# Sliding-window attention and Fourier mixing: the last chunk of the query-key projection at another rate, split straight from PSUM, and the first output-projection sets staged differently

## The chip, the cores and the metric

The kernel runs on one core of a Trainium2 chip. The metric is the device time of one execution in microseconds. PE is TensorE (matmuls; PEld its weight loads), ACT is ScalarE, DVE is VectorE, POOL is GpSimd, SP is SyncE, on whose queue all the DMAs named below are issued, in program order.

## The reference, cut to what matters

Four layers in turn on x (2048 x 640): attention, Fourier mixing, attention, Fourier mixing, each on a layer-normalized x and added to it.

```python
qkv = (x @ wqkv).reshape(B, S, 3, H, Dh)          # H = 32 heads, Dh = 20
scores = einsum("bhqd,bhkd->bhqk", q, k) * (Dh ** -0.5)
mask = (i - j >= 0) & (i - j < 256)
p = softmax(where(mask, scores, -1e9)); o = einsum("bhqk,bhkd->bhqd", p, v)
x = x + o.reshape(B, S, D) @ wo
...
y = dft_seq_re @ (x @ dft_hid_re.T) - dft_seq_im @ (x @ dft_hid_im.T); x = x + y
```

The change touches the attention layers alone, both of them alike.

## The kernel before, in words

Most large products are made with split operands: a float32 number becomes hi (rounded to the matmul type) plus lo (the rest), and three matmuls hi x hi, hi x lo, lo x hi make one product. `split` (L158) writes hi by ScalarE (L160) and lo by VectorE or GpSimd (L166).

**Head loop.** `heads` (L522) runs steps -10 to 128. Eight "quads" of four heads have 16 steps each, one for each block of 128 rows. A step makes four score products for the row maxima (`s_head`, L553, ten steps ahead: s = step + 10), whose masked maximum VectorE takes in place in PSUM (L558, three banks in turn), and four transposed score products (`t_head`, L578), which ScalarE turns into exponentials (L587) and GpSimd masks (L593, L597). `pv` (L608) multiplies the previous step's exponentials by the values. Every fourth step (94, 98, 102 and so on) `m_rows` transposes the maxima of four blocks, ScalarE copies them to `mt` (L567), and two small DMAs put them as row 61 into `qp` (L569), one tick later. The t_heads of the step four later are the first to need them. A step has two halves (z = 0, 1), and `tick` closes each: what was put off with `post(n, ...)` is issued n ticks later, what was put off with `defer(n, ...)` n steps later. Ticks set the order of the program only; the engines then run as their semaphores allow.

**Filler.** In the first half of a step `fill` (L671) puts in matmul pairs of other work, in this order:

- `project` (L490): the query and key projection, ten chunks of 128 columns. From step 0 on a chunk is made in two sets of two 512-column pieces, each set 30 pairs of matmuls with 64 rows (`lockstep`, L191). A chunk has 4 x 15 = 60 pairs, all ten 600. `fill` takes nf pairs a step, rounded so that a group of 15 comes out even; nf is RATE = 3.5, or more where a due time asks for it. `due` (L643) lists for each quad the pairs that must be done by a value of s; for the last quad 570 by s = 104 and 600 by s = 112. Quads are then loaded from DRAM by `pack` (L504), three DMAs a step.
- A finished piece is copied by ScalarE from PSUM (L477), cast and subtracted by GpSimd (L478, L479), and stored to DRAM (L456, 512 KB) six ticks after the copy.
- When the projection is at its end, `partials` (L852): the output projection for the first three of five chunks of the attention output (EARLY = 3; chunks 0 and 1 are heads 0 to 15, chunk 2 heads 16 to 23), 16 row blocks of 18 pairs (L191 again, 320 columns), nf = LATE = 9, so one block in two steps. It starts only when `early_o[0]["left"]` is 0. In the last steps and behind the loop the same work is made with full matmuls (`in_turn`, L173).

**Staging of the output projection.** `prepare(0)` runs ahead of the last chunk's first set: it loads the three weights. `prepare(2)` runs ahead of its second set: it splits them (hi on ScalarE, lo on GpSimd, 640 columns wide) and starts `load_o` (L743) for the first block of 512 rows. `load_o` loads a chunk of the attention output (L756, 256 KB) and, for a new range of heads, the reciprocal sums (L762, `rr`), posts GpSimd's scaling (L779) seven ticks later and the cut into hi and lo (L773) four ticks after that. `others` (L830) looks each step whether quad 5 has been stored and then loads chunks 1 and 2. `prepare(4)`, at the end of the projection, starts loading `y` (x in blocks of 128 x 640, L850), one a step for four steps. `stored` is set for a quad 14 ticks after its last pv.

**Behind the loop** the remaining partial products, then the last two chunks (`late`, L922), whose sums VectorE adds (L967), follow.

Of the kernel before, what the change touches and what calls it, by code (L numbers as in the profile page):

```python
# [7 lines left out]
F32 = mybir.dt.float32  # L8
# [9 lines left out]
P = 128  # L18
S = 2048
D = 640  # L20
# [6 lines left out]
NCH = 2 * D // P  # L27
# [6 lines left out]
EARLY = 3  # L34
AHEAD_X = 4
AFTER = 4
RATE = 3.5
FIRST = 7
LATE = 9
PACE = 0.65  # L40
SOON = 3
# [13 lines left out]
def cuts(ap, n):  # L55

    return [ap[:, i:i + n] for i in range(0, ap.shape[1] - n + 1, n)]
# [6 lines left out]
class Net:  # L64
# [66 lines left out]
    def next(self, name):  # L131
        i = self.turn.get(name, 0)
        self.turn[name] = i + 1
        tiles = getattr(self, name)[:3]
        return tiles[i % len(tiles)]
# [323 lines left out]
    def pieces(self, c, sbs, role):  # L459

        w = self.turn["w", c]
        sets, of = [], {}
        for sb in sbs:
            xt = self.xnt(sb)
            if sb % 2 == 0:
                sets.append(([], []))
            p = self.bank(role)
            of[id(p)] = p, sb, self.last_bank
            sets[-1][0].append(p)
            sets[-1][1].append([((w[:, 0, k, :], w[:, 1, k, :]), (xt[:, 0, k, :], xt[:, 1, k, :])) for k in range(KC)])  # L470

        lead = self.lead

        def copied(p, sb):
            st = self.work.tile([P, 2, 512], F32R, name="c", tag="c", bufs=3)
            r = self.raw()[:, :512]
            self.nc.scalar.activation(r, p, AF.Copy)  # L477
            self.post(1, lambda: self.nc.gpsimd.tensor_copy(st[:, 0, :], r))  # L478
            self.post(2, lambda: self.nc.gpsimd.tensor_tensor(  # L479
                out=st[:, 1, :], in0=r, in1=st[:, 0, :].bitcast(F32), op=OP.subtract))  # L480
            self.post(3 if lead else 6, lambda: self.store_qk(c, sb, st))
        for r in self.lockstep(sets):
            if isinstance(r, tuple):
                for p in r[1]:
                    p, sb, k = of[id(p)]
                    self.heavy.append((k, lambda p=p, sb=sb: copied(p, sb)))
                r = 0
            yield r
# [33 lines left out]
    def heads(self, xsrc, xdst, hook):  # L522
# [169 lines left out]
        for step in range(-LEAD, steps + 1):  # L692
            now[0] = step
            self.wide, self.lead, self.tiled = step + LEAD > steps, step < -2, step < steps - 1
            for f in later.pop(step, []):
                f()
            s, t, v = step + LEAD, step, step - 1
            if due and s >= due[0][0]:
                while done[0] < due[0][1]:
                    fill(15)  # L700
                due.pop(0)
                q, j = (s + AHEAD) // 16, (s + AHEAD) % 16 // 4
                for i, f in enumerate(self.pack(q, j)):
                    defer(i // 3, f)
                for f in later.pop(step, []):
                    f()
            if v >= 0 and v % 4 == 3:
                load_v(v // 4 + 2)
            if done[0] < total:
                nf = max([FIRST if t < 0 else RATE]  # L710
                         + [(d - done[0]) / max(1, at - s) for at, d in due])
            elif made[0] < early:
                nf = LATE
            else:
                nf = LATE
            rows = ((s - 1) // 16, ((s - 1) % 16) // 4) if 4 <= s < steps + 4 and s % 4 == 0 else None
            for z in range(2):
                for e in range(2):
                    heads = [(t_head, t, e), (s_head, s, 1 - e)]
                    for head, n, i in heads[::-1] if e else heads:  # L720
                        if 0 <= n < steps:
                            head(n // 16, n % 16, z, i)
                if 0 <= t < steps:
                    for e in range(2):
                        t_exp(t // 16, t % 16, z, e, e + 1)
                    t_mask(t // 16, t % 16, z)
                if z:
                    relieve()
                    if 0 <= v < steps:
                        pv(v // 16, v % 16)  # L730
                    if rows:
                        m_rows(*rows)
                if z == 0 and t >= 0 or t < -1 or t >= steps:
                    fill(nf)
                self.tick()
            if step > 16 * (NQ - 1):
                self.poll_late(step - 16 * (NQ - 1))
# [5 lines left out]
    def load_o(self, o, sb, k, raw=None, rr=None):  # L743
# [41 lines left out]
        if after:  # L785
            self.post(6, lambda: self.held.append(scale))
        else:
            self.post(7 if k < EARLY else 4 if sb == 2 else 6, scale)

    def let_go(self):  # L790
        held, self.held = self.held, []
# [16 lines left out]
    def prepare(self, n):  # L808

        nc, a = self.nc, self.a  # L810
        ks = range(EARLY)
        if n == 0:
            self.early_w = []
            raws = cuts(self.work.tile([P, 2 * D], F32, name="we", tag="wc"), D) + [None]
            self.early_l = [self.load_w(self.early_w, a["wo"], [k], at=k, eng=nc.gpsimd, into=raws[k]) for k in ks]
            for f in self.early_l:
                next(f)
        elif n == 2:
            self.take_big(0)
            self.early_w += pairs(cuts(self.big[0], D))[:EARLY]  # L820
            next(self.early_l[2])
            for i in range(2):
                self.defer(2 + 2 * i, lambda i=i: next(self.early_l[i]))
            self.take_big(1)
            oc = cuts(self.big[1], 512) + cuts(self.big[0][:, 6 * D:], 512)
            self.early_o = [dict(zip(ks, pairs(oc[:6]))), dict(zip(ks, pairs(oc[6:])))]
            self.early_o[0]["left"] = EARLY - 1
            self.load_o(self.early_o[0], 0, 0)

            def others():  # L830

                if (CHUNKS[EARLY - 1][1] // 4 - 1, 0) not in self.stored:
                    self.defer(1, others)
                    return
                for k in range(1, EARLY):
                    self.early_o[0]["left"] -= 1
                    self.load_o(self.early_o[0], 0, k)
            self.defer(1, others)
        elif n == 4:
            self.take_big(2, F32)  # L840
            for i in range(AHEAD_X):
                if i == 0:
                    self.load_y([i])
                else:
                    self.defer(i, lambda i=i: self.load_y([i]))
# [6 lines left out]
    def partials(self, xsrc):  # L852
# [4 lines left out]
        for t in range(NB):  # L857
# [3 lines left out]
            if i == 0:  # L861
                self.complete(sets[sb % 2])
            if sb + 1 < NSB and i == 0:
                for k in range(2):
                    self.load_o(sets[(sb + 1) % 2], sb + 1, k)
            ps = [self.bank("w" if self.wide else "m", 320) for _ in range(2)]
            terms = [self.out_terms(sets[sb % 2], w, ks, i, hf) for hf in range(2)]
            if self.tiled:
# [858 lines left out]
```

## Time and profile before

| | us |
|---|---|
| median of 3 runs (2180.86 to 2181.6) | 2180.93 |
| the profiled execution | 2180.11 |
| its span, first to last instruction | 2178.4 |

Mean granted TensorE clock of the profiled execution: 0.997. A row of the busy time by stretch reads: the stretch from the span's start and its length, then for PE, PEld, DVE, ACT and POOL the busy us with the number of instructions in brackets, then the granted clock, the mean busy share of the 16 DMA engines and their GB/s. Where it is asked for one line of code alone, only the engines that run that line have a column. A row in order of time reads: start, duration, engine, line, operation, output <- input, number merged, and in square brackets the idle time of the engine ahead of it with what ended it. A row of a group reads: line, engine, operation, output <- input, shapes, count | busy us, mean ns of one | idle us ahead of them, and what ended it.

### The profile page before, as it was taken

The numbers are of one execution on the slowest core, as the hardware profiler recorded it, in microseconds if no ns is written. First come the engines' busy times: TensorE is split into PE (matmuls) and PEld (weight loads), VectorE is DVE, ScalarE is ACT, GpSimd is POOL, SyncE is SP. The second block draws the span as 40 slices with busy tenths as digits, with TensorE's granted clock in tenths as the row PEclk, the third lists the DMA queues.
The fourth block names the chain that finished last, engine by engine and source line by source line (L and its number), as shares of the span: only waits on it lengthen the run. The fifth ranks groups of instructions, "written<-read, shape, count | busy, mean of one in ns | idle before, by whom it ended". The sixth has DMA issues, their size and how long they took to land.

```text
span 2178.4 us, 49193 instructions
## 1 busy us (share of the span) xinstructions
PE 2123.0 (97%) x17893; PEld 1777.4 (82%) x17893; DVE 1615.0 (74%) x3933; ACT 1150.3 (53%) x2483; POOL 930.8 (43%) x1458
## 2 busy tenths in 40 slices
PE   7999999899999999999999999998999999999999
PEld 7987777687878888889999877776877788888899
DVE  6348788786897868777751578886868878687777
ACT  3117777766554545543431277776665545455522
POOL 3037777875514223230130477777754333331300
PEclk9999999999999999999999999999999999999999
DMA  5546666786435454657646466667753454546653
GB/s 184 176 154 189 202 183 213 219 221 212 134 119 175 138 185 129 216 192 264 218 135 190 152 200 185 201 203 219 226 188 134 131 187 137 164 148 217 219 175 126
DMA packets 221618, 395.40 MB, mean 182 GB/s; under 512 B 39360, under 2 KB 85952, under 8 KB 221376
## 3 DMA queue, kind: packets, MB, share of 16 engines
q1 hardware_dynamic: 221376, 392.26, 57.0%
q8 instruction: 141, 2.31, 0.5%
q14 instruction: 101, 0.83, 0.1%
HBM read 273.94 MB, written 117.05 MB: 179 GB/s over the span
## 4 chain that ended last, share of the span: by engine, by line
PE 81%; DVE 6%; POOL 5%; ACT 4%; issue 2%; DMA 2%; SPq 0%; ACTq 0%; DVEq 0%; POOLq 0%
PE banks L1266 27%; PE banks L173 14%; PE banks L191 13%; PE banks L608 8%; PE banks L578 6%; PE banks L1521 6%; PE banks L553 4%; POOL big L166 1%; POOL ou L1196 1%; DVE qp L166 1%; ACT big L928 1%; PE banks L273 1%; DVE pt L1197 1%; POOL rs L978 1%; PE banks L565 1%
## 5 line engine op out<-in xcount | busy, mean ns | idle before, releaser
L558 DVE CUSTOM_DVE_ANT_0 banks<-banks,mask 128x384 f32<-128x384 f32 (+2 forms) x1024 | 526.8, 558 | 157.9 <-PE banks L553 119.3
L587 ACT ACTIVATE pt<-banks 128x384 f32<-128x384 f32 (+2 forms) x1024 | 430.5, 470 | 179.3 <-PE banks L553 95.4
L578 PE MATMUL banks<-qp,kp 61*128 61x384 f32 (+2 forms) x1024 | 310.6, 370 | 14.5 <-DMA qp<-mt 7.8
L593 POOL TENSOR_SCALAR_AFFINE_SELECT pt<-pt 128x256 f32<-128x256 f32 x512 | 212.8, 416 | 183.5 <-ACT pt L587 133.2
L553 PE MATMUL banks<-kp,qp 60*128 60x384 f32 (+2 forms) x1024 | 280.2, 360 | 1.4 <-DVE mc L558 1.1
L191 PE MATMUL banks<-big,wc 64*128 64x512 f32 x1920 | 269.6, 394 | 0.4 <-DVE pt L374 0.4
L578 PEld LDWEIGHTS banks<-qp,kp 61*128 61x128 f32 x1024 | 175.2, 185 | 79.9 <-ACT pt L587 35.3
L608 PE MATMUL banks<-pt,vq 128*32 128x128 f32 x5760 | 214.9, 278 | 2.9 <-POOL pt L593 2.9
L191 PEld LDWEIGHTS banks<-big,wc 64*128 64x128 f32 x1920 | 183.0, 185 | 28.0 <-ACT x L477 5.2
L608 PEld LDWEIGHTS banks<-pt,vq 128*32 128x32 f32 x5760 | 144.0, 109 | 57.5 <-issue 51.5
L597 POOL TENSOR_SCALAR_AFFINE_SELECT pt<-pt 128x256 f32<-128x256 f32 x448 | 186.5, 416 | 0.0
L1196 POOL TENSOR_TENSOR pt<-pt,pt 128x512 f32<-128x512 f32 x36 | 61.0, 1695 | 291.0 <-DMA pt<-c 245.6
L553 PEld LDWEIGHTS banks<-kp,qp 60*128 60x128 f32 x1024 | 161.3, 186 | 20.3 <-DVE mc L558 10.3
L160 ACT ACTIVATE c<-pt 128x512 fp32r<-128x512 f32 x150 | 93.5, 626 | 150.2 <-POOL pt L1172 52.5
L160 ACT ACTIVATE qp<-pt 128x512 fp32r<-128x512 f32 (+1 forms) x195 | 119.8, 624 | 90.4 <-DVE pt L1197 38.3
L166 DVE TENSOR_TENSOR qp<-pt,qp 128x512 fp32r<-128x512 f32 (+1 forms) x195 | 153.7, 801 | 11.9 <-ACT qp L160 8.9
L166 DVE TENSOR_TENSOR c<-pt,c 128x512 fp32r<-128x512 f32 x150 | 123.4, 833 | 50.1 <-ACT c L160 48.4
L1266 PE MATMUL banks<-qp,big 128*128 128x512 f32 x630 | 151.1, 391 | 5.1 <-DVE qp L166 4.1
L558 DVE DVE_READ_ACCUMULATOR2_ANT mc<- 128x1 f32 x1024 | 145.2, 142 | 0.0
L1266 PEld LDWEIGHTS banks<-qp,big 128*128 128x128 f32 x630 | 117.0, 188 | 31.1 <-DVE qp L166 5.7
L1266 PE MATMUL banks<-qp,xc 128*128 128x512 f32 x480 | 117.9, 390 | 1.8 <-DVE xc L166 1.5
L1266 PEld LDWEIGHTS banks<-qp,xc 128*128 128x128 f32 x480 | 89.8, 188 | 22.2 <-DVE xc L166 2.3
(224 smaller groups left out, 4362.3 us busy)
## 6 DMA issues: line engine op xcount, KB each, us to landing
pt<-c SPq DMA_DIRECT2D x188, 512.0 KB
qk_d<-c SPq DMA_DIRECT2D x80, 512.0 KB
kp<-qk_d SPq DMA_DIRECT2D x384, 80.0 KB
qp<-qk_d SPq DMA_DIRECT2D x384, 80.0 KB
kp<-u_d SPq DMA_DIRECT2D x32, 640.0 KB
o_d<-ou SPq DMA_DIRECT2D x64, 256.0 KB
x_d<-x SPq DMA_DIRECT2D x48, 320.0 KB
v_d<-pt SPq DMA_DIRECT2D x16, 768.0 KB
```

The lines of the kernel that those rows point to most:

```text
L160: nc.scalar.activation(hi, src, AF.Copy, scale=-1.0 if neg else 1.0)
L166: (eng or nc.vector).tensor_tensor(out=lo, in0=src, in1=hi.bitcast(F32), op=OP.subtract)
L173: self.nc.tensor.matmul(p, x, y, start=n == 0, stop=n == last)
L191: self.nc.tensor.matmul(ps[a], x[r], y[r], start=half + i == 0, stop=half == 1 and i == n - 1, skip_group_check=True)
L553: nc.tensor.matmul(p, qp[quad % 2][b:b + 60, z, qb * P:(qb + 1) * P], kp[quad % 2][b:b + 60, z, k0 * P:(qb + 1) * P], start=True, stop=True)
L558: nc.vector.tensor_tensor_reduce(out=p, in0=p, in1=self.mask[:, 384 - n * P:], scale=1.0, scalar=NEG, op0=OP.add, op1=OP.max, accum_out=mc ...
L578: nc.tensor.matmul(self.banks[:, e, :n * P], kp[quad % 2][b:b + 61, z, kb * P:(kb + 1) * P], qp[quad % 2][b:b + 61, z, kb * P:(kb + n) * P ...
L587: nc.scalar.activation(pt[quad, kb][:, 2 * z + e0:2 * z + e1, :n * P], self.banks[:, e0:e1, :n * P], AF.Exp, scale=SCALE)
L593: nc.gpsimd.affine_select(out=t[:, :, 0:P], in_=t[:, :, 0:P], pattern=[[0, 2], [1, P]], compare_op=OP.is_ge, fill=0.0, base=0, channel_mul ...
L597: nc.gpsimd.affine_select(out=t[:, :, 256:384], in_=t[:, :, 256:384], pattern=[[0, 2], [-1, P]], compare_op=OP.is_gt, fill=0.0, base=0, ch ...
L608: nc.tensor.matmul(p[32 * h:32 * h + 32, :], vq[:, 96 * (kb % 4) + 21 * h:96 * (kb % 4) + 21 * h + 32], t[:, h, (qb - kb) * P:(qb - kb + 1 ...
L1266: nc.tensor.matmul(self.banks[:, bk, :], p, b[q], start=start and m == 0, stop=stop and last and m == 2, skip_group_check=True)
```

## The change

- RATE holds until 540 of the 600 projection pairs are made; for the last 60, nf is LAST = 2.5 (or what a due time asks for).
- Pieces of the last chunk are split straight from PSUM by ScalarE and VectorE, and stored four ticks later. Pieces of the chunks before, from step -2 on, are stored eight ticks after the copy in place of six.
- The three early output weights are loaded in `prepare(0)` as before, but split in halves of 320 columns: the third at `prepare(2)` and two ticks later, the others two and four steps later, each in two halves.
- For the first 512 rows, chunk 0 of the attention output is loaded three steps after `prepare(2)` (before: at once), chunk 1 five steps after it, and chunk 2 from six steps after it on, when quad 5 has been stored (before: 1 and 2 together, from one step after it on). `left` stays above 0 until all three are cut.
- The scaling of chunk 2 of the first 512 rows is posted nine ticks after its load in place of seven.
- For the later 512 rows, chunk 1 is loaded two ticks after chunk 0 in place of at once.

```diff
+LAST = 2.5
...
+            if c == NCH - 1:
+                self.split(st[:, 0, :], st[:, 1, :], p)
+                self.post(4, lambda: self.store_qk(c, sb, st))
+                return
             r = self.raw()[:, :512]
             self.nc.scalar.activation(r, p, AF.Copy)
...
-            self.post(3 if lead else 6, lambda: self.store_qk(c, sb, st))
+            self.post(3 if lead else 8, lambda: self.store_qk(c, sb, st))
...
-                nf = max([FIRST if t < 0 else RATE]
+                nf = max([FIRST if t < 0 else RATE if done[0] < total - 4 * per_piece else LAST]
                          + [(d - done[0]) / max(1, at - s) for at, d in due])
...
-            self.post(7 if k < EARLY else 4 if sb == 2 else 6, scale)
+            self.post((9 if sb == 0 and k == EARLY - 1 else 7) if k < EARLY else 4 if sb == 2 else 6, scale)
...
-            raws = cuts(self.work.tile([P, 2 * D], F32, name="we", tag="wc"), D) + [None]
-            self.early_l = [self.load_w(self.early_w, a["wo"], [k], at=k, eng=nc.gpsimd, into=raws[k]) for k in ks]
-            for f in self.early_l:
-                next(f)
+            self.early_r = cuts(self.work.tile([P, 2 * D], F32, name="we", tag="wc"), D) + [self.raw()]
+            for k in ks:
+                nc.sync.dma_start(self.early_r[k], a["wo"][:, k, :])
+
+            def halves(k):
+                for i in range(2):
+                    cs = slice(320 * i, 320 * i + 320)
+                    (hi, lo), r = self.early_w[k], self.early_r[k]
+                    self.post(2 * i, lambda hi=hi[:, cs], lo=lo[:, cs], r=r[:, cs]: self.split(hi, lo, r, eng=nc.gpsimd))
+            self.halves = halves
...
-            next(self.early_l[2])
+            self.halves(2)
             for i in range(2):
-                self.defer(2 + 2 * i, lambda i=i: next(self.early_l[i]))
+                self.defer(2 + 2 * i, lambda i=i: self.halves(i))
...
-            self.early_o[0]["left"] = EARLY - 1
-            self.load_o(self.early_o[0], 0, 0)
+            self.early_o[0]["left"] = EARLY
...
-                for k in range(1, EARLY):
-                    self.early_o[0]["left"] -= 1
-                    self.load_o(self.early_o[0], 0, k)
-            self.defer(1, others)
+                another(EARLY - 1)
+
+            def another(k):
+                self.early_o[0]["left"] -= 1
+                self.load_o(self.early_o[0], 0, k)
+            self.defer(3, lambda: another(0))
+            self.defer(5, lambda: another(1))
+            self.defer(6, others)
...
-                for k in range(2):
-                    self.load_o(sets[(sb + 1) % 2], sb + 1, k)
+                o = sets[(sb + 1) % 2]
+                self.load_o(o, sb + 1, 0)
+                o["left"] += 1
+
+                def another(o=o, n=sb + 1):
+                    o["left"] -= 1
+                    self.load_o(o, n, 1)
+                self.post(2, another)
```

## The prediction, made before the changed kernel was run

> **What bounds the kernel now.** The page's first lines come first.
>
> ```profile
> span 2178.4 us, 49193 instructions
> PE 2123.0 (97%) x17893; PEld 1777.4 (82%) x17893; DVE 1615.0 (74%) x3933; ACT 1150.3 (53%) x2483; POOL 930.8 (43%) x1458
> ```
>
> PE is busy nearly everywhere, so a gain has to come from the few places where it is not. I looked for them with the busy time by stretch, cutting at whole steps of the head loop (a step is the four products of L578). 323.0 begins step 60, 366.0 step 76, 410.6 step 92, 423.6 step 97, 429.6 step 98, 435.1 step 99, and 524.0 ends step 127; the second attention repeats them at 1447.3, 1491.8, 1504.9, 1511.3 and 1516.8. Behind the busy times stand granted clock, DMA share and GB/s.
>
> ```profile
> 323.00:366.00 43.00, 42.89 (x616) 32.47 (x612) 35.23 (x133) 32.69 (x83) 31.65 (x71) 1.00 0.63 195
> 366.00:410.60 44.60, 43.33 (x618) 32.71 (x614) 35.33 (x133) 34.41 (x86) 36.78 (x74) 1.00 0.70 215
> 410.60:423.60 13.00, 11.26 (x165) 7.01 (x161) 11.17 (x42) 9.05 (x25) 11.39 (x22) 1.00 0.85 244
> 423.60:429.60 6.00, 1.88 (x22) 1.01 (x17) 2.37 (x10) 3.06 (x7) 4.89 (x9) 0.89 0.82 270
> 429.60:435.10 5.50, 5.50 (x45) 4.42 (x45) 2.39 (x9) 2.19 (x5) 1.47 (x4) 0.50 0.64 193
> 435.10:524.00 88.90, 88.35 (x1372) 72.03 (x1375) 62.03 (x199) 60.88 (x150) 64.79 (x126) 1.00 0.73 206
> 1447.30:1491.80 44.50, 43.23 (x616) 32.55 (x612) 35.21 (x133) 34.33 (x85) 36.70 (x74) 1.00 0.70 215
> 1491.80:1504.90 13.10, 11.36 (x165) 7.05 (x161) 11.28 (x43) 9.12 (x25) 11.49 (x22) 1.00 0.81 229
> 1504.90:1511.30 6.40, 1.80 (x20) 0.95 (x17) 2.34 (x10) 3.06 (x7) 4.85 (x9) 0.92 0.88 273
> 1511.30:1516.80 5.50, 5.48 (x43) 4.44 (x43) 2.39 (x9) 2.12 (x5) 1.41 (x4) 0.50 0.69 190
> ```
>
> Steps 92 to 96 last 13.00 / 5 = 2.60 us, those of 60 to 75 last 43.00 / 16 = 2.69, steps 99 to 127 last 88.90 / 29 = 3.07. But step 97 lasts 6.00 with PE busy for 1.88, and step 98 lasts 5.50 at a clock of 0.50. The same view for L191 alone gives the filler matmuls, two to a pair:
>
> ```profile
> 366.00:410.60 44.60, 17.46 (x120) 11.59 (x120) 1.00 0.70 215
> 410.60:429.60 19.00, 0.00 (x0) 0.00 (x0) 0.96 0.84 252
> 429.60:435.10 5.50, 2.79 (x18) 2.71 (x18) 0.50 0.64 193
> ```
>
> So 60 pairs in steps 76 to 91, **none in six steps**, then nine a step. A step without filler is only 0.09 us shorter than one with 3.75 pairs: it is bound by its chain of score, exponential and mask, and an empty step throws PE time away. Two waits stand out. The first, in step 85, from the order of time (POOL, PE):
>
> ```profile
> 386.81 0.61 POOL L478 CAST c<-x 128x512 fp32r<-128x512 f32 x1
> 388.31 1.31 POOL L479 TENSOR_TENSOR c<-x,c 128x512 fp32r<-128x512 f32 x1
> 390.84 1.62 POOL L166 TENSOR_TENSOR big<-x,big 128x640 fp32r<-128x640 f32 x1
> 392.38 1.31 POOL L479 TENSOR_TENSOR c<-x,c 128x512 fp32r<-128x512 f32 x1
> 394.10 0.41 PE L608 MATMUL banks<-pt,vq 128*32 128x128 f32 x4 [1.16 <-POOL pt L593]
> ```
>
> The mask (L593) stands behind two pieces of the last chunk and a whole output weight. The second is step 97's; the SyncE queue and PE in order of time:
>
> ```profile
> 412.72 1.69 SPq L756 DMA_DIRECT2D x<-o_d  x2
> 414.53 0.52 SPq L762 DMA_DIRECT2D rr<-r_d  x1
> 415.72 0.43 SPq L850 DMA_DIRECT2D big<-x  x1
> 417.62 0.36 SPq L850 DMA_DIRECT2D big<-x  x1
> 418.92 0.25 ACT L567 ACTIVATE mt<-banks 16x128 fp32r<-16x128 f32 x1
> 419.59 0.38 SPq L456 DMA_DIRECT2D qk_d<-c  x1
> 421.06 0.33 SPq L850 DMA_DIRECT2D big<-x  x1
> 423.31 0.39 SPq L456 DMA_DIRECT2D qk_d<-c  x1
> 423.79 1.48 SPq L569 DMA_DIRECT2D qp<-mt  x2
> 429.56 0.65 PE L578 MATMUL banks<-qp,kp 61*128 61x384 f32 x1 [3.66 <-DMA qp<-mt]
> ```
>
> The row maxima of step 94 are ready at 418.92 + 0.25 = 419.17, but their DMA starts at 423.79, behind bulky transfers on one queue, and PE gets them 10.4 us after they were ready; it wanted them after 6.7. This stretch is full:
>
> ```profile
> 416.00:426.00 10.00, 8.59 (x117) 5.02 (x113) 8.52 (x32) 6.87 (x20) 7.87 (x18) 1.00 1.00 300
> ```
>
> **The change, part by part.** Nothing before step 76 moves except the stores of the earlier chunks, two ticks (one step) later; their readers (pack) come at least five steps behind, so I cost it at nothing. If that cover failed, pack's loads would wait at a due step.
>
> *Rate.* From 540 of 600 pairs on, a group of 15 goes in five steps of three, not four of 4, 4, 4, 3. The due times ask for at most (600 - 540) / (112 - 86) = 2.3 a step (the loop's s is the step plus 10), so 2.5 rules. The last chunk fills steps 76 to 95. The second set, and prepare(2) with it, comes at step 86, not 84. The early sets are loaded at steps 89, 91 and 92 (quad 5's store at step 91 is still the gate); their scalings run at 92, 94 and 96 (nine ticks for the last) and their cuts at 94, 96 and 98. Partial products start at step 99, not 98. **Empty steps: 96 to 98, three in place of six.**
>
> Per pair a step costs (43.00 - 16 x 2.60) / 60 = 0.023 us. Sixteen steps with 48 pairs: 41.6 + 1.1 = 42.7. Four with 12: 10.4 + 0.3 = 10.7. Three empty: 7.8. Together 61.2 us for steps 76 to 98, if neither wait comes back. Before: 44.60 + 13.00 + 6.00 + 5.50 = 69.1, and 69.5 in the second attention. Gain **7.9 and 8.3, sum 16.2**.
>
> *One step less for partial products.* Nine of K=64 pairs, the work of nine full matmuls, slide past the loop. Their price, from full ones there, and DVE behind them:
>
> ```profile
> 528.42 2.84 PE L173 MATMUL banks<-qp,kp 128*128 128x320 f32 x18
> 530.00:548.00 18.00, 14.57 (x80) 12.11 (x79) 17.62 (x46) 11.58 (x21) 8.47 (x10) 1.00 0.72 235
> ```
>
> Nine of 18 in 2.84 is 1.42 us each attention. DVE is busy for 17.62 of 18 us afterwards, so a later start may be partly made up (0) or not (1.42). I take 1.42, since DVE's first operation there needs those products: **+2.8**.
>
> *Pieces split from PSUM.* The groups by line, form kept apart:
>
> ```profile
> L479 POOL TENSOR_TENSOR c<-x,c 128x512 fp32r<-128x512 f32 x64 | 83.6, 1308 | 0.6
> L478 POOL CAST c<-x 128x512 fp32r<-128x512 f32 x64 | 39.2, 616 | 33.6 <-ACT x L477 33.5
> L477 ACT ACTIVATE x<-banks 128x512 f32<-128x512 f32 x64 | 38.2, 604 | 55.0 <-PE banks L191 41.0 <-issue 12.8
> L160 ACT ACTIVATE big<-banks 128x512 fp32r<-128x512 f32 x32 | 19.1, 596 | 55.3 <-PE banks L273 55.3
> L166 DVE TENSOR_TENSOR big<-banks,big 128x512 fp32r<-128x512 f32 x32 | 22.0, 686 | 23.9 <-ACT big L160 23.9
> L166 POOL TENSOR_TENSOR big<-we,big 128x640 fp32r<-128x640 f32 x4 | 6.3, 1571 | 0.0
> ```
>
> ScalarE's part stays (604 against 596 ns). POOL loses 4 x (0.616 + 1.308) = 7.7 us per attention and DVE gains 4 x 0.686 = 2.74, and each subtraction waits for ScalarE's half first. Behind it in DVE's order stand the score reductions (L558), whose end frees PE's score banks, and the next group's first filler now waits for two readers of its bank in place of one. DVE is busy 35.23 of 43.00, so most fits into its gaps: between 0 and 2.74 I take a quarter, 0.7: **+1.4**. Bound from below: in these steps POOL could also run ahead and give something back.
>
> The Trainium skill speaks against this move: "Perfetto Trace Analysis", section Optimizing Scalar/DVE Operations, says that GpSimd and DVE share an SBUF port and that moving work between the two might not help. If each DVE subtraction held POOL for its length, POOL would still win 1.924 - 0.686 per piece. No row of before shows the two against each other here; the rival "step 85 stays" stands for it.
>
> *Weights in halves* (1.571 us as two of half the width, at steps 86, 88, 90) delay a mask by about 0.8 us instead of 1.62. POOL's time is free: it was busy 31.65 of 43.00 in quiet steps. Steps 94 and 96 each still get a scaling beside a cut. *One scaling later* costs nothing: it only keeps the third scaling from the second.
>
> *What is late next.* The transfers ahead of the maxima of step 98, needed by step 102: three y loads (128 x 640 x 4 = 320 KB) and two stores (512 KB), 1984 KB. Before, for step 94, there were also two x (256 KB each) and rr (256 KB): 768 KB more, at 300 GB/s 2.6 us. So about 10.4 - 2.6 = 7.8 us from ready to landed, against 6.7 + 3 x (3.07 - 2.60) = 8.1 allowed, since steps 99 to 101 are longer. It fits narrowly, with the stores one step further ahead of the maxima.
>
> **Sum.** -16.2 + 2.8 + 1.4 = -12.0 on the profiled execution's 2180.1 (span 2178.4 and 1.7 around it): 2168.1. The median of the runs, 2180.9, is 0.8 above it: **2168.9 us**.
>
> **Rivals.** *A smaller wait at step 102*: 2.5 us in each attention, too short to drop the clock: 2168.9 + 5.0 = 2173.9. For it: the narrow margin. Against: before, the maxima of step 98 also had some 1 MB of loads ahead of them (y, x, rr, x of the first partial product), and steps 99 to 127 lose only 88.90 - 88.35 of PE. A wait of 1.16 us in step 85 left the clock at 1.00; one of 3.66 was followed by 0.50. The Trainium skill, "TensorE: Matmul & The Clock Gate", Part 1, states that an idle window of about 3.4 us halves the clock, and the two rows agree.
>
> *Step 85 stays* (POOL or DVE late after all): its 44.60 - 43.00 = 1.6 us remain and DVE's 2.74 show in full: 2 x (1.6 + 2.0) = 7.3, 2176.2.
>
> *The change doesn't do what it says*: the maxima's wait moves to step 102 whole. It cost 6.00 + 5.50 - 2.60 - 3.07 = 5.8, and 6.2 in the second attention: 12.0 more, 2180.9, within 0.2%.
>
> *Slower*: the same wait, grown. Without the pause in step 97 the queue keeps filling: y loads and stores at 96 to 98, then x, rr, x, x, rr (1280 KB) at 99 and 100. If the maxima come w us late at step 102 or 106, an attention loses w + 5.50 - 3.07 for the clock. From w = 3.6 the gain is gone, from 5.8 it is slower by 0.2%; at w = 7, 2 x 9.4 = 18.8: 2187.7.
>
> **How the numbers follow.** Forecast 0.58, smaller wait 0.18, step 85 stays 0.06, whole wait 0.09, grown wait 0.09. A measurement here can tell about 0.2% (4.4 us) from no change: faster means below 2176.5. Faster: 0.58 + 0.17 + 0.05 = 0.80; within: 0.11; slower: 0.09. The forecast's own range: 2163.8 (costs of DVE and tail at nothing, and 0.9 for steps 97 and 98 quicker than 2.60) to 2173 (DVE's 2.74 in full). The range reaches over the two next cases to 2176.5 and leaves out 0.18.
>
> **What would show it.** Right: L191 in steps 76 to 95 at six matmuls a step; three steps empty; no wait of PE for qp<-mt; clock 1.00 from step 76 to 127; no wait of L608 for POOL in step 85; nine full L173 matmuls more after the loop. Wrong: a wait for qp<-mt at step 102 or 106, L553 waiting for DVE at 85 and 95, or partial products that start after step 99.

## The result, and the profile after

| | us |
|---|---|
| after, median of 6 runs (2187.84 to 2193.17) | 2189.81 |
| before, median of 6 runs (2179.15 to 2182.16) | 2181.22 |
| ratio, 95% interval | 1.0041, [1.0031, 1.0051] |
| the profiled execution of after, the slowest of the six; its span | 2193.17; 2191.3 |

Slower by 0.4%, where 2168.9 was forecast. The page of after begins so:

```profile
span 2191.3 us, 49195 instructions
PE 2135.2 (97%) x17857; PEld 1784.3 (81%) x17857; DVE 1613.2 (74%) x3941; ACT 1150.3 (52%) x2489; POOL 924.5 (42%) x1448
```

PE's busy time rose by 12.2 us over that of before with 36 matmuls fewer: they ran slower. The busy time of after by stretch shows where (clock, DMA share and GB/s are the last three columns). In the first attention 367.8 begins step 76, 421.7 step 96, 430.3 step 99, 436.5 step 101, 443.2 step 102, 448.2 step 103, 458.0 step 105, 469.5 step 108, and 531.2 ends step 127.

```profile
367.80:421.70 53.90, 53.19 (x745) 38.22 (x741) 44.15 (x166) 41.07 (x108) 39.72 (x87) 1.00 0.70 201
421.70:430.30 8.60, 6.81 (x79) 4.06 (x75) 8.24 (x30) 6.96 (x17) 6.95 (x14) 1.00 0.59 176
430.30:436.50 6.20, 6.20 (x103) 5.16 (x102) 4.74 (x17) 3.90 (x11) 3.88 (x9) 1.00 0.95 272
436.50:443.20 6.70, 3.33 (x54) 2.57 (x51) 3.04 (x12) 2.19 (x6) 2.31 (x6) 1.00 0.86 254
443.20:448.20 5.00, 4.98 (x53) 4.13 (x53) 2.15 (x11) 1.87 (x5) 0.77 (x2) 0.66 0.95 253
448.20:458.00 9.80, 6.72 (x101) 5.33 (x100) 4.83 (x18) 4.47 (x11) 6.00 (x10) 0.99 0.86 219
458.00:469.50 11.50, 11.43 (x153) 9.45 (x151) 7.36 (x26) 7.23 (x17) 8.89 (x17) 0.86 0.71 183
469.50:531.20 61.70, 61.13 (x914) 49.31 (x914) 40.60 (x118) 41.58 (x104) 44.78 (x85) 1.00 0.69 198
```

Steps 76 to 98 last 62.5 us (before 69.1): that part of the forecast came. Then step 101 lasts 6.70 us with PE busy for half of it, step 102 runs at 0.66, and steps 103 and 104 lose 3.1 us more. Steps 99 to 107 together last 39.2 us, where before took 28.3 for as many PE instructions (x453 in both); in the second attention it is 35.6 against 28.5. Before:

```profile
435.10:463.40 28.30, 28.29 (x453) 23.22 (x452) 21.77 (x81) 19.36 (x47) 20.31 (x41) 1.00 0.74 203
```

The filler alone (L192, the old L191) followed the plan:

```profile
367.80:421.70 53.90, 18.36 (x120) 11.55 (x120) 1.00 0.70 201
421.70:430.30 8.60, 0.00 (x0) 0.00 (x0) 1.00 0.59 176
430.30:433.50 3.20, 1.49 (x18) 1.39 (x18) 1.00 0.93 303
```

The waits of PE and GpSimd in the whole kernel (total, times, longest), after and then before:

```profile
PE banks L613 <- POOL pt L598: 8.7, 8, 2.2
PE banks L583 <- DMA qp<-mt: 4.3, 2, 3.4
PE banks L558 <- DVE mc L563: 3.5, 8, 0.6
POOL x L784 <- DMA rr<-r_d: 17.3, 8, 4.8
```
```profile
PE banks L578 <- DMA qp<-mt: 7.8, 2, 4.2
PE banks L608 <- POOL pt L593: 2.9, 4, 1.2
PE banks L553 <- DVE mc L558: 1.1, 2, 0.5
POOL x L779 <- DMA rr<-r_d: 0.5, 1, 0.5
```

The wait for the maxima (qp<-mt) halved, but GpSimd's scaling (L784) now stands 17.3 us waiting for the reciprocal sums. The SyncE queue of after shows how both came about:

```profile
415.27 0.35 SPq L639 DMA_DIRECT2D r_d<-rc  x1
415.66 0.73 SPq L761 DMA_DIRECT2D x<-o_d  x1
418.31 0.52 SPq L767 DMA_DIRECT2D rr<-r_d  x1
...
425.04 1.12 SPq L574 DMA_DIRECT2D qp<-mt  x2
...
429.69 0.38 SPq L864 DMA_DIRECT2D big<-x  x1
430.17 0.37 SPq L457 DMA_DIRECT2D qk_d<-c  x1
...
432.59 0.56 SPq L864 DMA_DIRECT2D big<-x  x1
433.25 0.39 SPq L457 DMA_DIRECT2D qk_d<-c  x1
...
437.94 2.74 SPq L574 DMA_DIRECT2D qp<-mt  x2
...
444.05 0.59 SPq L767 DMA_DIRECT2D rr<-r_d  x1
...
450.19 0.52 SPq L767 DMA_DIRECT2D rr<-r_d  x1
```

The maxima of step 94, ready at 419.75, left at 425.04, 5.3 us late, *before* any y load or last store: rr of chunk 2 had stood 1.8 us until the sums just written to `r_d` were in DRAM (the queue's own waits, 410 to 460 us):

```profile
SPq L767 <- DMA r_d<-rc: 1.8, 1, 1.8
```

Those of step 98, ready at 430.75, left at 437.94 and 440.16 (the second inside the 2.74). rr of the next block left at 444.05 and landed at about 450.3. What that did, in order of time on PE and then on GpSimd:

```profile
443.22 0.41 PE L583 MATMUL banks<-qp,kp 61*128 61x384 f32 x1 [3.39 <-DMA qp<-mt]
452.00 0.41 PE L613 MATMUL banks<-pt,vq 128*32 128x128 f32 x4 [0.85 <-POOL pt L598]
457.66 0.46 PE L613 MATMUL banks<-pt,vq 128*32 128x128 f32 x4 [2.23 <-POOL pt L598]
```
```profile
450.31 1.28 POOL L784 TENSOR_TENSOR x<-x,rr 128x512 f32<-128x512 f32 x1 [4.76 <-DMA rr<-r_d]
451.54 0.41 POOL L598 TENSOR_SCALAR_AFFINE_SELECT pt<-pt 128x256 f32<-128x256 f32 x1
...
455.98 1.26 POOL L784 TENSOR_TENSOR x<-x,rr 128x512 f32<-128x512 f32 x1 [1.69 <-DMA rr<-r_d]
457.20 0.41 POOL L598 TENSOR_SCALAR_AFFINE_SELECT pt<-pt 128x256 f32<-128x256 f32 x1
```

The masks (L598) stand in GpSimd's order behind a scaling, in steps 103 and 104, whose result the partial products need only from step 107 on, and PE waits for the masks.

### The profile page after: what moved, and what is told of

It is laid out like the page before. It is cut to its first block, busy times and chain, and to the rows that moved or that the text cites. A ratio compares the mean times of both kernels' runs of the same rounds, so it can differ in the third digit from the quotient of the medians.

```text
span 2191.3 us, 49195 instructions
## 1 busy us (share of the span) xinstructions
PE 2135.2 (97%) x17857; PEld 1784.3 (81%) x17857; DVE 1613.2 (74%) x3941; ACT 1150.3 (52%) x2489; POOL 924.5 (42%) x1448
## 4 chain that ended last, share of the span: by engine, by line
PE 81%; DVE 6%; POOL 4%; DMA 4%; ACT 3%; issue 2%; SPq 1%; POOLq 0%; DVEq 0%; ACTq 0%
PE banks L1286 29%; PE banks L174 14%; PE banks L192 13%; PE banks L613 8%; PE banks L583 6%; PE banks L1541 6%; PE banks L558 4%; DMA rr<-r_d 2%; POOL big L167 1%; ACT big L948 1%; POOL ou L1216 1%; DVE qp L167 1%; DMA kp<-qk_d 1%; POOL rs L998 1%; PE banks L274 1%
## 5 line engine op out<-in xcount | busy, mean ns | idle before, releaser
L583 PE MATMUL banks<-qp,kp 61*128 61x384 f32 (+2 forms) x1024 | 316.7, 374 | 7.1 <-DMA qp<-mt 4.3
L598 POOL TENSOR_SCALAR_AFFINE_SELECT pt<-pt 128x256 f32<-128x256 f32 x512 | 213.3, 417 | 191.4 <-ACT pt L592 125.7
L558 PE MATMUL banks<-kp,qp 60*128 60x384 f32 (+2 forms) x1024 | 283.0, 363 | 4.8 <-DVE mc L563 3.5
L192 PE MATMUL banks<-big,wc 64*128 64x512 f32 x1920 | 271.4, 394 | 1.3 <-DVE c L167 0.9
L192 PEld LDWEIGHTS banks<-big,wc 64*128 64x128 f32 x1920 | 183.2, 186 | 28.0 <-ACT x L482 4.5
L1216 POOL TENSOR_TENSOR pt<-pt,pt 128x512 f32<-128x512 f32 x36 | 66.1, 1835 | 301.1 <-DMA pt<-c 195.9
L558 PEld LDWEIGHTS banks<-kp,qp 60*128 60x128 f32 x1024 | 161.5, 187 | 24.4 <-DVE mc L563 14.3
L161 ACT ACTIVATE c<-pt 128x512 fp32r<-128x512 f32 x150 | 93.5, 626 | 145.2 <-POOL pt L1192 52.1
L161 ACT ACTIVATE qp<-pt 128x512 fp32r<-128x512 f32 (+1 forms) x195 | 119.8, 624 | 86.9 <-DVE pt L1200 34.8
L167 DVE TENSOR_TENSOR c<-pt,c 128x512 fp32r<-128x512 f32 x150 | 124.3, 838 | 53.0 <-ACT c L161 51.2
```

Source lines behind the costliest of these rows:

```text
L161: nc.scalar.activation(hi, src, AF.Copy, scale=-1.0 if neg else 1.0)
L167: (eng or nc.vector).tensor_tensor(out=lo, in0=src, in1=hi.bitcast(F32), op=OP.subtract)
L192: self.nc.tensor.matmul(ps[a], x[r], y[r], start=half + i == 0, stop=half == 1 and i == n - 1, skip_group_check=True)
L558: nc.tensor.matmul(p, qp[quad % 2][b:b + 60, z, qb * P:(qb + 1) * P], kp[quad % 2][b:b + 60, z, k0 * P:(qb + 1) * P], start=True, stop=True)
L583: nc.tensor.matmul(self.banks[:, e, :n * P], kp[quad % 2][b:b + 61, z, kb * P:(kb + 1) * P], qp[quad % 2][b:b + 61, z, kb * P:(kb + n) * P ...
L598: nc.gpsimd.affine_select(out=t[:, :, 0:P], in_=t[:, :, 0:P], pattern=[[0, 2], [1, P]], compare_op=OP.is_ge, fill=0.0, base=0, channel_mul ...
```

## The experiments

Counted over both attentions of each profiled execution; the waits are totals: PE for maxima (mt), the scaling for rr, PE for masks. "First" is the first step with partial products. Each ratio is to before in the same session, whose median lay between 2179.95 and 2181.41 us; the step columns are of one execution, which can lie off the median (after: its slowest; e18: its fastest, 2178.93).

| run | us | ratio to before, 95% | first | steps 76-95 | 96-107 | 108-127 | mt | rr | masks |
|---|---|---|---|---|---|---|---|---|---|
| before | 2181.22 | | 98 | 109.9 | 85.4 | 121.1 | 7.8 | 0.5 | 2.9 |
| after | 2189.81 | 1.0041 [1.0031, 1.0051] | 99 | 107.8 | 93.5 | 126.5 | 4.3 | 17.3 | 8.7 |
| e1 | 2191.88 | 1.0045 [1.0029, 1.0062] | 99 | 115.2 | 86.9 | 124.2 | 6.5 | 4.7 | 1.1 |
| e2 | 2178.00 | 0.9989 [0.9979, 1.0000] | 98 | 107.5 | 84.8 | 121.0 | 0 | 2.8 | 8.7 |
| e5 | 2190.93 | 1.0039 [1.0024, 1.0054] | 99 | 107.2 | 92.7 | 124.3 | 0 | 10.0 | 13.6 |
| e6 | 2185.58 | 1.0020 [1.0010, 1.0030] | 99 | 107.8 | 88.1 | 123.4 | 0.7 | 7.4 | 5.8 |
| e9 | 2186.89 | 1.0027 [1.0016, 1.0038] | 99 | 107.8 | 87.2 | 125.2 | 0 | 9.9 | 5.6 |
| e10 | 2190.73 | 1.0039 [1.0024, 1.0054] | 99 | 108.8 | 91.8 | 124.7 | 1.9 | 16.5 | 8.4 |
| e11 | 2193.73 | 1.0054 [1.0037, 1.0070] | 99 | 107.7 | 94.9 | 124.4 | 0.5 | 16.8 | 9.7 |
| e14 | 2182.67 | 1.0002 [0.9992, 1.0011] | 98 | 107.5 | 88.0 | 121.2 | 1.8 | 5.7 | 2.5 |
| e17 | 2186.07 | 1.0032 [1.0023, 1.0041] | 99 | 109.8 | 85.2 | 125.1 | 6.8 | 4.0 | 4.0 |
| e18 | 2182.16 | 1.0010 [1.0001, 1.0019] | 98 | 106.5 | 85.9 | 121.7 | 2.2 | 6.3 | 3.0 |
| e19 | 2187.43 | 1.0035 [1.0022, 1.0048] | 99 | 108.1 | 85.7 | 127.6 | 0 | 1.6 | 9.5 |
| e20 | 2191.10 | 1.0047 [1.0033, 1.0061] | 99 | 107.7 | 90.8 | 124.2 | 1.0 | 17.3 | 9.7 |
| e21 | 2181.54 | 1.0012 [1.0003, 1.0021] | 98 | 107.4 | 85.7 | 124.6 | 0 | 1.1 | 9.3 |

**The rate: undone in after (e1), alone in before (e2).**

```diff
-RATE if done[0] < total - 4 * per_piece else LAST    # e1: RATE throughout; e2: the reverse, in the kernel before
```


> The changed kernel with the last chunk at 3.5 pairs a step again, all else as changed. Queue theory (SyncE's queue lags, and the row maxima and rr stand in it behind the y loads, the last stores and the loads of the second set): the y loads and last stores go out at steps 92 to 95 again, well ahead of step 99; PE's wait for qp<-mt under 1 us, POOL's wait for rr under 1 us, steps 99 to 127 about 89 us again, total 2168 to 2174. DVE theory (the loss comes from the subtractions put on VectorE and from the banks they hold): those stay, total within 3 us of the changed kernel's 2190.

> The kernel before with only the rate of the last chunk at 2.5. Queue theory: the rate alone moves the y loads and the last stores next to the second set's loads; waits for qp<-mt and rr in steps 98 to 106 of 8 us or more an attention, total 2188 or more. DVE theory: no subtraction was moved, so nothing of the loss appears, and with half the empty steps the total is 2172 to 2178.

The theory formed from the trace of after, that the rate itself brings y and the stores next to the loads of the next block and so is the loss, is refuted twice: without the rate after is no faster, and the rate alone is no slower than before. Both times fit the rival DVE theory (e2 at the very edge of its range), which e5 tests below. In e1 PE waits for the maxima at the end of step 97 again, 5.3 us; in e2 that wait is gone, but the masks' wait grew from 2.9 to 8.7 and steps 96 to 107 take 84.8 us against 85.4. **The wait changed its place and its engine; little of it went.**

**Other queues: the maxima (e3), y (e4) issued by ScalarE.**

```diff
-nc.sync.dma_start(qp[...], mt[...])        # e3: nc.scalar.dma_start
-self.nc.sync.dma_start(self.y_part(t), ...) # e4: self.nc.scalar.dma_start
```


> The changed kernel with the two small DMAs of the row maxima issued by ScalarE, which makes the maxima, in place of SyncE. Queue theory: they no longer stand behind the bulky transfers, PE's waits for qp<-mt (3.4 and 0.9 us) go, the clock holds 1.00 to step 102, POOL's waits for rr stay; total 2181 to 2186. Theory of full DMA engines (the transfers themselves are late, whatever queue they stand in): the maxima land as late as now, total 2189 or more.

> The changed kernel with all y loads (16 of 320 KB an attention) issued by ScalarE in place of SyncE. Queue theory: SyncE's lag at step 98 falls by at least 3 us, the waits for qp<-mt and rr shrink to less than half; total 2174 to 2182. Theory of full DMA engines: as many bytes in the same steps, the waits stay within 1 us of now, total 2188 to 2191.

Both much slower than either theory had it: 2281.91 us (1.0464 [1.0442, 1.0485]) and 2228.68 us (1.0219 [1.0204, 1.0235]). SyncE's own waits, in e3 (whole kernel) and then in e4 (410 to 470 us, steps 92 to 105 of the first attention):

```profile
SPq L515 <- DMA qp<-mt: 115.6, 51, 5.8
```
```profile
SPq L515 <- DMA big<-x: 14.3, 3, 7.8
SPq L574 <- DMA big<-x: 3.5, 1, 3.5
```

By these rows SyncE's loads now wait until DMAs of the *other* queue have landed. The scalings' wait for rr grew to 44.1 and 28.4 us. Moving a DMA to another queue did not make the SyncE queue shorter.

**One part of after undone at a time: split (e5), early loads (e9), stores (e10), the later load (e11).**

```diff
-if c == NCH - 1: self.split(...); self.post(4, ...); return   # e5: left out
-self.defer(3, lambda: another(0)) ...                         # e9: chunk 0 at once, 1 and 2 together from the next step
-self.post(3 if lead else 8, ...)                              # e10: 6
-self.post(2, another)                                         # e11: another()
```


> The changed kernel, but the pieces of the last chunk go by GpSimd again (copied by ScalarE, cast and subtracted by GpSimd, stored eight ticks later). Three theories stand. Loads theory (the early loads of chunks 0 and 1 were moved from step 86 to steps 89 to 92, into the stretch where the SyncE queue already lags; the maxima of steps 94 and 98 then leave 5.3 and 7.2 us late where the kernel with the rate alone has 2.2 and 3.7): the split is not the cause, 2186 to 2192 us, and PE waits for qp<-mt at step 101 as in the changed kernel. Split theory (DVE's subtractions make the steps longer and the stores come earlier on the queue): 2176 to 2181 us, as with the rate alone, no wait for qp<-mt. Store theory (stores eight ticks after the copy stand right ahead of the maxima): 2186 to 2192 us.

> The changed kernel, but chunk 0 of the attention output is loaded at once in prepare(2) again, and chunks 1 and 2 together from one step after it on, when quad 5 has been stored. Loads theory: the maxima of steps 94 and 98 leave at most 3 and 4.5 us late, no wait of PE for qp<-mt at step 101, 2174 to 2181 us. Split theory and store theory: the waits stay, 2186 to 2192 us.

> The changed kernel, but the pieces of the chunks before the last are stored six ticks after the copy again. Store theory: the 5.0 us that the maxima of step 82 leave late fall back to about 2.5, the queue is not behind from there on, 2177 to 2183 us. Loads theory and split theory: the lag at step 82 may shrink, but that of steps 94 and 98 stays above 5, 2186 to 2192 us.

> The changed kernel, but chunk 1 of the later blocks of 512 rows is loaded right behind chunk 0 again, not two ticks later. A fourth theory, that this order makes GpSimd's scalings wait for rr (9.5 us in four waits in the second attention) and so the masks and PE behind them: 2181 to 2185 us, no wait of the scaling for rr<-r_d above 1.5 us. Loads, split and store theory: 2186 to 2192 us.

Each theory's number misses in the run that undoes its own part (split 2176 to 2181 us, loads 2174 to 2181, stores 2177 to 2183, the fourth 2181 to 2185). The early loads are a part: with them as before, the maxima of step 94 leave 2.8 us late instead of 5.3, no wait for them is left, the rr wait falls to 9.9, but the time falls only by 2.9 us (the intervals overlap). Stores, later load and split, undone alone, change nothing that can be told.

**Traffic or order: y two blocks ahead (e6), later scalings (e13).**

```diff
-AHEAD_X = 4                                # e6: 2
-... else 7) if k < EARLY ...               # e13: later blocks 10, their chunk 2: 8
```


> The changed kernel, but y (x in blocks of 128 x 640) is loaded two blocks ahead instead of four, so that 640 KB of the 1984 KB ahead of the maxima of step 98 go later. Traffic theory (behind the projection the transfers of y, two stores, x and rr follow each other without a pause, and whichever is wanted first is late): the maxima of step 98 leave at most 5 us late instead of 7.2, no wait of PE for qp<-mt at step 101, 2183 to 2187 us. Order theory (GpSimd stands in a scaling that waits for rr, and the masks behind it hold PE): the wait for qp<-mt may go, but the scalings' wait of 4.8 us and that of PE for the masks stay, 2187 to 2191 us.

> The changed kernel, but the scalings of the later blocks of 512 rows are posted ten ticks (chunk 2: eight) behind their loads instead of seven. Order theory: no wait of a scaling for rr above 1 us, PE's waits for the masks (8.7 us in the whole kernel) fall below 3, 2183 to 2187 us. Traffic theory: the wait for qp<-mt and the lower clock behind it stay, and what the masks win is small, 2187 to 2191 us.

e6 met the traffic theory in time and in PE's wait: 640 KB fewer in the stretch take 4.2 us off (the intervals are just apart). The lag of the maxima of step 98 fell from 7.2 to 5.5 us in the first attention, not to 5. In the second attention steps 96 to 103 run almost clean; at step 104 the scaling's wait is still there. e13 (part of its later scalings multiply by the reciprocal sums of another set) took 2212.14 us, 1.0142 [1.0125, 1.0159]: steps 102 to 104 fell to 9.7 us, but then PE waited 11.3 us for the cuts that now came too late. It decides nothing.

**Parts built up from before: scaling at nine ticks (e17), rate and split (e18), rate, split and halves (e14); eight ticks in after (e20).**

```diff
+9 if sb == 0 and k == EARLY - 1 else 7    # e17, in before; e20: 8 for 9, in after
+if c == NCH - 1: self.split(...); ...     # e18 and e14, with LAST = 2.5; e14 also halves(k)
```


> The kernel before with one change, the scaling of chunk 2 of the first 512 rows posted nine ticks after its load. Phase theory (of the two ticks one is free, the second puts the cut behind the filler of step 98, so that partial products start a step later and half a block out of step with the maxima): partial products from step 99 or one later than before, steps 108 to 127 in 61.7 us instead of 60.5, nine pairs fewer in the loop; 2 x (1.2 + 1.4) = 5.2 us, 2184 to 2188 us, less if the wait of step 97, which is over before partial products start, swallows the step. If it is free, as forecast: 2180 to 2182 us.

> The kernel before with the rate and the split from PSUM alone. Split theory (VectorE's subtractions make steps 86 and 96 1.1 us longer each and cover what GpSimd wins): 2181 to 2184 us, as with the weights in halves too (2182.7). Halves theory (the split is even or better and the halves cost): 2176 to 2179 us.

> The kernel before with the rate, the pieces split from PSUM and the weights in halves alone (loads, stores, scalings and the later load of chunk 1 as before). Phase theory (the scaling two ticks later costs a step: partial products start at step 99 in every kernel that has it, and at 98 in those that have not; from then on each two steps of a block stand otherwise to the four steps of the maxima, and steps 108 to 127 last 61.7 us instead of 60.5, with nine pairs a step fewer): partial products from step 98, steps 108 to 127 in 60.5 us, and with the nine matmuls 2180 to 2183 us. Split theory (VectorE's part of the split is why the kernel with the early loads as before, 2186.9 us, stands 9 us above that with the rate alone): 2185 to 2188 us.

> The changed kernel, but the late scaling is posted eight ticks after its load instead of nine. Phase theory: partial products start at step 98, steps 108 to 127 last 60.5 us again, 2183 to 2186 us. If the early loads or the waits behind step 99 set the start, it stays at step 99 and 2187 to 2192 us.

**The scaling alone costs 0.32%** (2186.07 us, within the 2184 to 2188 of the phase theory). Two ticks put its cut behind the filler of step 98, and so does one tick (e20 starts at 99 too, against the expectation). A block takes two steps, so from 99 on a block would begin in step 127 and not end there: the step gets nine full matmuls in place of 18 with 64 rows, and an attention's loop has 504 of the latter, not 540. The stretch of steps 108 to 127 (first attention, or both), in before, e14, e17:

```profile
463.40:524.00 60.60, 60.05 (x923) 48.81 (x923) 40.26 (x119) 41.52 (x104) 44.48 (x85) 1.00 0.72 208
```
```profile
464.30:524.85 60.55, 59.99 (x923) 48.75 (x923) 40.20 (x119) 41.62 (x104) 44.48 (x85) 1.00 0.72 204
```
```profile
463.30:526.74 63.44, 61.40 (x915) 49.48 (x914) 40.89 (x118) 41.15 (x104) 44.79 (x85) 1.00 0.68 195
1548.70:1610.44 61.74, 61.17 (x914) 49.23 (x914) 40.48 (x118) 41.17 (x104) 44.88 (x85) 1.00 0.69 197
```

The work is the same (nine full matmuls do that of 18 with 64 rows), yet it takes 1.2 us longer or more in every kernel that starts at 99. Step 127 itself makes 0.4 us of it (2.13 for 1.76). That the later start brings it is shown by e17, whose only edit acts ahead of step 99; which conflict makes the rest, and that it is one step against the maxima's four, is not shown. After itself with partial products from step 98 was not run.

The split on top of the rate takes 0.9989 to 1.0010 (intervals just apart); the halves add nothing (1.0010, 1.0002). So the split costs about 4 us. e5 does not show it: there GpSimd has its pieces back, and the masks' wait rises from 8.7 to 13.6 while that for the maxima goes (4.3 to 0).

**Attempts to keep the rate's gain: e15, e19, e21, e22**, before with the rate and later scalings.

```diff
+e15: y two ahead, later blocks 10, their chunk 2: 8      # e19: first chunk 2 at 8, later chunks 0, 1 at 9
+e21: later chunks 0, 1 at 9                              # e22: the same with y two ahead
```


> The kernel before with the rate, y two blocks ahead, and the scalings of the later blocks ten ticks (chunk 2: eight) behind their loads. By the traffic theory and the order theory together the waits at steps 97, 103 and 104 go: steps 96 to 107, 42.5 us with the rate alone, come to about 38, 2168 to 2174 us. If the gain of the rate is taken back wherever it is made: 2176 to 2180 us.

> The kernel before with the rate, chunk 2 of the first 512 rows scaled eight ticks after its load, and chunks 0 and 1 of the later blocks nine ticks after theirs, chunk 2 of them seven as before. Order theory: the scaling's wait for rr (2.4 us with the rate alone) and the longer steps 103 and 104 (2.0 us in an attention) go, partial products still start at step 98, and steps 105, 113 and 121 stay as with the rate alone: 2172 to 2176 us. Traffic theory: the time comes back at another step, 2177 to 2180 us.

> The kernel before with the rate, and chunks 0 and 1 of the later blocks of 512 rows scaled nine ticks after their loads; everything of the first 512 rows as before (in the kernel with the eighth tick partial products had started a step late, at 99, which hid what the later scalings do). Order theory: partial products from step 98, no wait of a scaling for rr, steps 102 to 104 in 9.6 us instead of 11.6 and 11.4, 2172 to 2176 us. Traffic theory: what the scaling no longer waits for, another step waits for, 2177 to 2181 us.

> The same with y loaded two blocks ahead instead of four. Order theory: within 2 us of the same kernel with y four ahead, 2172 to 2177 us. Traffic theory: the 640 KB that go later are what counts, 3 us or more below it.

e15: 2180.39 us, 0.9995 [0.9985, 1.0004]; e22: 2182.87 us, 1.0011 [1.0002, 1.0020]. e19 misses both its ranges, since its eighth tick put the start at 99. The order theory **falls as the whole cause**: in e21 the scaling waits 1.1 us in place of 2.8, steps 102 to 104 lose their excess in part (10.9 and 10.7 us for 11.6 and 11.4), and steps 108 to 127 lose 3.6 us again, because the later scalings and cuts then meet steps 113 and 119 to 121. PE's wait for masks stays at 9.3: GpSimd's own pieces, scalings and cuts make it, not rr alone. The rate alone (e2) stays the fastest kernel, and its interval reaches 1.0000.

## Why the prediction was wrong, point by point

- **Rate and empty steps: right in count.** Six matmuls a step, three empty steps, 62.5 and 63.9 us for steps 76 to 98 against 61.2. But e2 shows that the 16.2 us were mostly the end of waits, and these came back elsewhere: alone it is worth about 2.4 us.
- **The step that failed is "What is late next".** It put the next waits at nothing, and steps 99 to 107 took 18.0 us more than before (74.8 for 56.8). It took from the 10.4 us of before only the bytes that no longer stood ahead of the maxima (7.8 us against 8.1 allowed); measured are 12.4, from 430.75 to 443.2. Those 10.4 us came from a queue that was 0.3 us behind at the maxima of step 90. In after it was 5.3 us behind at step 94 already, in part by the staged early loads (2.8 without the staging, e9), which the same prediction had moved to steps 89 to 92 and costed at nothing. And it asked about the maxima alone; the rr of the next block, with the masks in GpSimd's order behind its scaling, was in none of the cases. That the pause of 6 us in step 97 had given these loads their time before is a reading; no run shows it by itself.
- **"One scaling later costs nothing": wrong**, some 5 us by the medians (e17). The start at step 99 was in the sum, but not put down to this edit. Its price was sized wrong both ways. An attention has 36 full matmuls of partial products, 18 before; nine of the 18 more stand in step 127, and nine slide behind it, as forecast. But they cost nothing there, not 1.42 us: from the end of step 127 to step 60 of the second attention it is 880.3 us before and 880.4 after. The 1.2 us in steps 108 to 127 was not foreseen.
- **The split: mis-sized.** About 4 us by the medians (e18 against e2), not 1.4. In after step 86 is 1.1 us longer than before and step 96 too, in each attention, where 0.7 was put down for both; in step 96 two pieces are subtracted. DVE in step 96 of after, in order of time, and its group, beside the stretch (from 421.70, 3.70 us, in the second attention the same):

```profile
421.38 0.69 DVE L167 TENSOR_TENSOR c<-banks,c 128x512 fp32r<-128x512 f32 x1 [0.47 <-POOL pt L598]
421.99 0.56 DVE L563 CUSTOM_DVE_ANT_0 banks<-banks,mask 128x384 f32<-128x384 f32 x1
...
422.98 0.69 DVE L167 TENSOR_TENSOR c<-banks,c 128x512 fp32r<-128x512 f32 x1
423.58 0.56 DVE L563 CUSTOM_DVE_ANT_0 banks<-banks,mask 128x384 f32<-128x384 f32 x1
```
```profile
421.70:425.40 3.70, 2.56 (x36) 1.45 (x32) 3.70 (x13) 2.79 (x6) 2.07 (x4) 1.00 0.71 214
```

  DVE is busy for all of it, and PE's wait for it (L558) grew from 1.1 to 3.5 us. Where the rest of the 4 us goes is open: in e18's one profiled execution, its fastest, steps 76 to 98 are even shorter than in e2 (64.8 us for 65.6), and PE waits for the masks 3.0 us in the whole kernel in place of 8.7. On the port that GpSimd and DVE share ("Perfetto Trace Analysis", section Optimizing Scalar/DVE Operations, of the Trainium skill): neither was slowed by the other here. The masks that ran beside a whole subtraction took 409 to 414 ns (417 on average, 416 before), and DVE's subtractions 685 to 692 (686 before).
- **Empty steps at full clock: wrong in the second attention**, see the last section; about 3 us there.
- **Step 85's wait goes, halves and stores cost nothing: right** (steps 84 to 87 in 12.0 us for 12.7; e14, e10).
- **The rivals.** "Grown wait" had the place (the wait ends at 443.2, the start of step 102) and nearly the time (2187.7), but only a part of the mechanism: 3.4 of 7 us, the rest through GpSimd, so that its time is near is partly luck. It was given 0.09 because the pause in before was read as waste alone.

Of the 12.9 us between the two profiled spans 11.4 lie in steps 76 to 127 (316.4 us before, 327.8 after): -2.1 to step 95, +8.1 in steps 96 to 107, +5.4 in steps 108 to 127. Most of the rest lies ahead of step 0, whose start varies from 160.7 to 164.4 us between kernels. How the 8.1 divides between early loads, split and start cannot be told apart, since each of these moves the others' waits. As an estimate from the ratios: the rate alone (0.9989), the split (+0.0021), the halves (-0.0008), the scaling (+0.0032) and the early loads (+0.0014, after against e9) add up to 1.0048; measured is 1.0041.

## What to carry to other kernels

A pause of the busiest engine can also be time in which queues catch up: before counting it as gain, list *all* that was issued during it, with the time each is wanted, and start the sum from how far the queue is behind at that point, read from a row such as that of the maxima (ready against issued), not from zero. Look for instructions that wait for a load and stand in an in-order engine ahead of work that the busiest engine needs at once; to put them later gained nothing here (e21), as they then met other steps. Moving an operation by a tick can make all that it feeds start a whole step later: look up which filler slot its consumer then misses.

## What the runs showed of the hardware

The clock fell without a long wait. In after, step 96 is alike in both attentions, yet in the second the clock halved. The stretches of steps 96, 97, 98 and 99 there, and below them the stretch at 0.50 with the 3.41 us ahead of it:

```profile
1508.80:1512.50 3.70, 2.56 (x38) 1.44 (x34) 3.70 (x13) 2.73 (x6) 2.07 (x4) 1.00 0.74 201
1512.50:1515.20 2.70, 2.45 (x20) 1.23 (x16) 2.25 (x9) 2.11 (x5) 2.70 (x6) 0.52 0.48 155
1515.20:1518.80 3.60, 3.38 (x31) 1.96 (x27) 2.71 (x11) 2.36 (x7) 2.92 (x6) 0.50 0.57 168
1518.80:1523.60 4.80, 4.80 (x53) 4.17 (x52) 2.04 (x7) 2.16 (x6) 1.68 (x6) 0.58 0.95 276
1509.20:1512.61 3.41, 2.27 (x34) 1.40 (x34) 3.41 (x12) 2.38 (x6) 1.83 (x3) 1.00 0.71 200
1512.61:1522.85 10.24, 9.77 (x71) 6.69 (x75) 6.14 (x24) 6.05 (x15) 7.08 (x15) 0.50 0.69 211
```

The longest wait of PE in steps 96 to 99 is 0.64 us, but PE is busy for only 2.56 of 3.70 in step 96. Before, five empty steps with PE busy for 11.26 of 13.00 us kept 1.00. So sparse work, not one long gap, went with the drop here. The gap of 2.23 us at step 104 was also followed by half clock.

The trace's clock shows how the same step can end in two ways. In after the head loops' four stretches at 0.50 begin at 444.24, 457.89, 1512.61 and 1574.05 and last 3.41, 3.41, 10.24 and 3.41 us, and their starts lie 4, 309 and 18 times 3.413 us apart. On this grid, PE was busy for 2.27 of the 3.41 us ahead of the drop at 1512.61. In the first attention step 96 lies across two stretches of the grid with 2.77 and 2.52 us (from 420.35 and 423.76), and the clock stayed. No threshold can be read from it: before, a stretch with 2.25 us (from 390.69) kept 1.00. That such luck of position makes the spread of e18's runs (2178.93 to 2186.91) is not shown.

The Trainium skill ("TensorE: Matmul & The Clock Gate", Part 1) speaks of one idle window of about 3.4 us, free-running. The grid agrees with that length, but the windows ahead of these two drops were not idle (PE busy for 2.27 and 1.18 us), and the measurement decides.

A DMA on SyncE's queue waited for DMAs that another engine had issued to land (e4: 7.8 us at the longest), and a load of what a store had just written stood 1.8 us at the head of the queue, with all behind it.
